# Scheduler thresholds as a string of settings along the run, in a planned attention and MLP kernel

## The chip, the cores and the metric

The kernel runs on one core of one Trainium2 chip. The metric is the device time of one execution in microseconds (us). Three runs of the kernel before gave 1594.99, 1595.41 and 1596.77 us; the median, 1595.41, is the time before.

The engines are named as in the profile: PE is TensorE (matrix products; PEld is its loading of weights), ACT is ScalarE, DVE is VectorE, POOL is GpSimd and SP is SyncE, which issues the DMAs.

## What is computed

The reference, cut to what matters. The sequence has 2048 tokens of 512 values, and there are 32 heads of 16 values.

```python
def _A_ref(x, wqkv, wo):
    H = 32; Dh = D // H
    qkv = (x @ wqkv).reshape(B, S, 3, H, Dh).transpose(2, 0, 3, 1, 4)
    q, k, v = qkv[0], qkv[1], qkv[2]
    p = _softmax(jnp.einsum("bhqd,bhkd->bhqk", q, k) * Dh ** -0.5)
    o = jnp.einsum("bhqk,bhkd->bhqd", p, v)
    return o.transpose(0, 2, 1, 3).reshape(B, S, D) @ wo

def _B_ref(x, w1, b1, w2, b2):               # w1: 512 x 1376, w2: 1376 x 512
    h = _gelu(jnp.einsum("bsd,df->bsf", _layernorm(x), w1) + b1)
    return jnp.einsum("bsf,fd->bsd", h, w2) + b2

x = x + _A_ref(_layernorm(x), wqkv, wo)
x = x + _B_ref(_layernorm(x), w1, b1, w2, b2)
x = x + _A_ref(_layernorm(x), wqkv, wo)
x = x + _B_ref(_layernorm(x), w1, b1, w2, b2)
```

Each attention needs an exponential of 32 x 2048 x 2048 scores. In tiles of 128 keys by 512 queries of one head that is 16 x 4 x 32 = 2048 tiles, and 4096 for both.

## The kernel before

**A planner writes the program.** The Python code doesn't list the instructions of each engine in order. It runs a list scheduler, `Sched`, over a model of the chip: every operation has a duration, and every engine a time at which it is free (`P.free`). Jobs are generators that yield tasks with a priority (a lower number goes first). `Sched.run` picks, over and over, the task that can start first (`best`, L389), and appends its instructions to the engine's stream. The streams are then emitted with the semaphore waits that the dependences need. So the order on each engine is fixed when the program is built, and the thresholds at L477 to L509 are arguments of that planning: they are read by the planner and are not on the chip. A change of one threshold at one point can change the order of all that follows.

**Segments and tiles.** The attention is cut into segments (`build_segments`): one block of queries for one group of four heads. A segment has its score tiles, and the tiles of the key blocks in `DK` (3, 6, 9, 12 and 15) are kept in a list of their own, `todod`, because they may go to DVE. These are 5 of 16 key blocks, 1280 of the 4096 tiles.

**Two ways to an exponential.** ACT takes groups of tiles. `flow_scores` (L1319) forms them by turns with three tiles (PSUM banks 0 to 2) and two tiles (banks 3 and 4); before the run is `wide`, in the first part, both have two. PE writes the scores of a group (L1401), ACT reads all banks of it in one instruction (L1386) and writes bf16 probabilities into one of nine sets of `PT` (five with three tiles, four with two). The counter `gi` numbers the groups. DVE takes a tile alone: an addition of a constant to the score, rounded to a 16-bit integer, gives the bits of an approximate exponential (`d_load`, L1478). Two such tiles share one buffer `dp`, and three more additions (`job_d`, L1509) make copies shifted by quarter powers of two. All four copies are multiplied with V scaled to match (`vs`), which averages the error out. A tile on ACT thus needs one product with V, and a tile on DVE four.

**Which tile goes to DVE** is decided by `take_d` (L1411). It needs DVE not too far behind, room in `dp`, a free PSUM bank (bank 5, `DLANE`, or bank 7, `MISCB`), and a tile in `todod` whose operands are there. It is asked in three places: by `flow_scores` beside each group, by `d_solo` after each DVE instruction that is planned (L1458, when the DVE work at hand is at most `D_IDLE`), and when PE has a gap. Tiles of `todod` that nobody has taken when a segment's other tiles are done go to ACT.

**Products with V** are batched by `try_pv` (L1526). It considers probabilities that are ready within `PV_NEAR`, takes one or two from each of the four heads, and gives the batch a value: the number taken over 4 (r + 0.5), with r the depth, at most 2. If the value is below `PV_LEAST` it holds the batch back, until PE has been drained for `PV_IDLE` (0.5 us), a set of `PT` is lacking (`starved`), or the segment's last tiles are due.

**Scores go first on PE.** When a score task is expected soon, `scores_due` (L417) gives a due time, and `best` passes over any other PE task that would drain more than `HOLD_LATE` after it.

**Linear layers** (QKV L927, output projection L1658, the MLP L1713 and L1756) run beside the attention, at their own priorities, in pieces of two matmuls; products with V have priority 1.0 and scores 0.0. They share PSUM bank 7.

When all is planned, `refill` (L1202) goes through the plan once more and puts matmuls with a tile of zeros (`zw`, L1307, L1309, L1311) into PE's gaps.

Of the kernel before, what the change touches and what calls it, by code (L numbers as in the profile page):

```python
# [38 lines left out]
DK = (3, 6, 9, 12, 15)  # L39
# [239 lines left out]
class Sched:  # L279
# [137 lines left out]
    def scores_due(self, f, lim):  # L417

        first = None
        for t in self.pend["pe"]:  # L420
            if t.prio == 0.0:
                r = self.task_ready(t)
                if r > lim and (first is None or r < first):
                    first = r
        if first is None or first - f > HOLD_REACH:
            return None
        act = self.P.free["act"] + sum(max(0.02, o[4] - OVERLAP["act"]) for t in self.pend["act"] for o in t.ops)
        return max(first, act - HOLD_LEAD) + HOLD_LATE

    def drained(self, task, t):  # L430

# [45 lines left out]
AHEAD = 0.3  # L477
HOLD_REACH = 1.0
HOLD_LEAD = 0.45
HOLD_LATE = 0.4  # L480
FILL_GAP = 0.2
FILL_LEAST = 96
FILL_MOST = 448
# [6 lines left out]
GELU_FROM = 0.3  # L490
GELU_TO = 0.5
DLANE = 5
D_IDLE = 1.2
D_NEAR = 0.5
D_PRIO = 0.5
DBATCH = 2
# [5 lines left out]
MISCB = 7  # L502
DTAIL = 8
DURGE = 8
PV_NEAR = 0.7
PV_DEEP = 2
PV_COST = 0.5
PV_LEAST = 0.75
PV_IDLE = 0.5  # L509


class Builder:
# [380 lines left out]
    def job_qkv_tile(self, L, tt, slot, i, left, prio, what):  # L893
        S_ = self.S_
# [8 lines left out]
        xnT, RXT = self.xnT[:, xs, :, :], ("xnT", xs)  # L903
# [20 lines left out]

        def mm(which, b):
            for c0 in (0, 2):
                yield Task("pe", prio, [I(lambda e, c=c: e.matmul(self.ps[:, b, :], lhsT=xnT[:, c, :], rhs=self.wqkv[:, c, which * 512:which * 512 + 512], start=(c == 0), stop=(c == 3)),  # L927
                                          [("wqkv", which), RXT], [("ps", b)], 0.216, [("ps", b)]) for c in (c0, c0 + 1)])
        yield ("ready", "pe", [RXT])
        if "k" in what:  # L930
# [388 lines left out]
    def flow_scores(self):  # L1319
# [4 lines left out]
        self.batch = None  # L1324
        self.ptuse = {}
        self.lane_busy = False
        self.dload = 0
        for b in range(4):
            S_.retire("mb", b, ("ret", b))
        last = {}  # L1330
        while True:
            self.advance()
            if self.cur == len(self.segs):
                break
# [35 lines left out]
            while self.wide and len(grp) + len(dts) < 4:  # L1370
                d = self.take_d([s_["tiles"][j][1] for s_, j in grp] + [s_["tiles"][j][1] for s_, j, b, bt, w in dts])
                if d is None:
                    break
                dts.append(d)
            ops = []
            for (sg, j), b in zip(grp, banks):
                ops.append(self.score(sg, j, b))
# [30 lines left out]
        while self.cur < len(self.segs) and not self.left(self.segs[self.cur]):  # L1408
            self.cur += 1

    def take_d(self, hps):  # L1411

        S_, P = self.S_, self.P
        self.advance()
        if self.cur == len(self.segs) or self.dload > 1 or P.free["dve"] - S_.now > 1.3 or sum(o[4] for t in S_.pend["dve"] for o in t.ops) > DBACK:
            return None
        if self.batch is None and (not S_.pools["dp"].free or S_.pools["dp"].waiters or self.flying >= DFLY):
            return None
        mb = S_.pools["mb"]
        soon = lambda b: P.ready("pe", (), [("ps", b)]) <= max(S_.now, P.free["pe"]) + 0.1  # L1420
        if not self.lane_busy and ("ret", DLANE) in S_.done and soon(DLANE):
            b = DLANE
        elif MISCB in mb.free and not mb.waiters and soon(MISCB):
            b = MISCB
        else:
            return None
        sg = self.segs[self.cur]
        if self.left(sg) < DTAIL:
            if self.cur + 1 == len(self.segs):
                return None  # L1430
            sg = self.segs[self.cur + 1]
            if sg["nt"] - self.left(sg) >= (DAHEAD if ("retq", 5) in S_.done else DAHEAD // 2):
                return None
        if not sg["todod"]:
            return None
        j = next((j for j in sg["todod"] if sg["tiles"][j][1] not in hps), sg["todod"][0])
        kbs = sg["tiles"][j][0]
        if not all(k in self.S_.done for k in [("qt", sg["i"])] + self.kv_keys(sg, kbs) + [("vs", sg["i"], kb) for kb in kbs]):
            return None
        if b == DLANE:  # L1440
            self.lane_busy = True
        else:
            mb.free.remove(b)
        self.dload += 1
        sg["todod"].remove(j)
        sg["n"] += len(SHIFT) - 1
        bt = self.batch
        if bt is None:
            bt = self.batch = {"unit": S_.pools["dp"].free.pop(0), "tiles": [], "loaded": 0, "closed": False}
            self.ptuse[("dp", bt["unit"])] = 1  # L1450
            self.flying += 1
        w = len(bt["tiles"])
        bt["tiles"].append((sg, j))
        if w + 1 == DBATCH:
            self.batch = None
        return (sg, j, b, bt, w)

    def d_solo(self):  # L1458

        S_ = self.S_  # L1460
        if not self.wide or self.P.free["dve"] - S_.now + sum(o[4] for t in S_.pend["dve"] if S_.task_ready(t) <= S_.now + D_NEAR for o in t.ops) > D_IDLE:
            return
        d = self.take_d([])
        if d is not None:
# [61 lines left out]
    def try_pv(self):  # L1526
        S_ = self.S_
        while True:
# [2 lines left out]
            sg = self.segs[self.acc_seg]  # L1531
            if self.pv_out >= (1 if self.pv_first else 2) or not sg["rdy"]:
                return
            near = [it for it in sg["rdy"] if self.P.last_writer[it[2]].t1 <= S_.now + PV_NEAR]
            if len(near) < len(sg["rdy"]):
                S_.seq += 1
                heapq.heappush(S_.timers, (min(self.P.last_writer[it[2]].t1 for it in sg["rdy"] if it not in near) - PV_NEAR + 0.01, S_.seq, self.try_pv))
            if not near:
                return
            by = defaultdict(list)  # L1540
# [124 lines left out]
    def job_post(self, L, qc):  # L1665
# [43 lines left out]
    def mm_w1(self, L, qc, fc, b, pr, W, off=0):  # L1709
        M = 128 if fc < self.NFC - 1 else self.FLAST  # L1710
        yield ("keys", [("w1", L, qc, fc)])
        for c0 in (0, 2):
            yield Task("pe", pr, [I(lambda e, c=c: e.matmul(self.ps[0:M, b, off:off + W], lhsT=self.w1(fc, c), rhs=self.yT[:, c, 0:W], start=(c == 0), stop=(c == 3)),  # L1713
                                    [("wf", fc)] + [("yT", i) for i in range(W // 128)], [("ps", b)], 0.216 * W / 512, [("ps", b)]) for c in (c0, c0 + 1)])

    def gt(self, fc, i, W):
# [4 lines left out]
    def job_ffn(self, L, qc):  # L1721
# [30 lines left out]
        for i, tt in enumerate(tiles):  # L1752
            yield ("ready", "pe", GR + [r for fc in range(NFC) for r in self.w2res(L, fc)])
            b = yield ("get", "mb")
            for f0 in range(0, NFC, 2):
                yield Task("pe", pr, [I(lambda e, fc=fc, i=i, b=b: e.matmul(self.ps[:, b, :], lhsT=self.gt(fc, i, W), rhs=self.w2(L, fc), start=(fc == 0), stop=(fc == nf)),  # L1756
                                        GR + self.w2res(L, fc), [("ps", b)], 0.216, [("ps", b)]) for fc in range(f0, min(f0 + 2, NFC))])
            S_.submit(Task("dve", pr - 0.7, [I(lambda e, tt=tt, b=b: e.tensor_tensor(out=self.xres[:, tt, :], in0=self.ps[:, b, :], in1=self.xres[:, tt, :], op=ALU.add), [("ps", b), ("x", tt)], [("x", tt)], 0.68)]),
                      cb=lambda b=b, tt=tt: self.x_done(L, tt, b, pr))
# [179 lines left out]
```

## Time and profile before

| | |
|---|---|
| median of three runs | 1595.41 us |
| the profiled execution's own time | 1595.76 us |
| its span, first to last instruction | 1594.1 us |
| PE busy, with the zero matmuls | 1538.6 us (97%) |
| ACT busy | 1528.0 us (96%) |
| DVE busy | 1450.3 us (91%) |
| POOL busy | 333.9 us (21%) |
| exponential groups on ACT | 1274, first at 24.8 us, last at 1571.3 us |
| tiles on DVE | 944, first at 90.3 us, last at 1558.8 us |

A row for a group of instructions has the line, the engine and the operation, then what it writes and reads with the shapes, the count, the busy time in us, the mean duration of one in ns, and last the idle time of the engine just before these instructions with what ended it. A row of waits has the engine and line that waited, the one waited for, and the time in total, how often, and the longest. A row of the timeline begins with the start and the busy time of a run of equal instructions; in brackets is the idle time before it.

### The profile page before, as it was taken

To read this page: it belongs to the slowest core of one execution; us is meant where nothing else is said; L and a number is where in the kernel's file an instruction comes from. 1 tells how busy PE (TensorE), PEld (TensorE's weight loads), DVE (VectorE), ACT (ScalarE), POOL (GpSimd) and SP (SyncE) were. 2 spreads that over 40 slices of the span, in tenths; PEclk is the share of its full clock that TensorE was granted. 3 is DMA by queue.
4 is the path that set the end of the run, shared out by engine and by line. 5 is a ranking of instruction groups with operands and counts; after the bars stand their busy time and mean duration, and the time that the engine had idled before them with its cause. 6 is when DMAs were issued, how large, how long until landed. Compare 5 with 4: busy or idle time off the path is not lost.

```text
span 1594.1 us, 39159 instructions
## 1 busy us (share of the span) xinstructions
PE 1538.6 (97%) x16364; PEld 479.4 (30%) x16497; DVE 1450.3 (91%) x3202; ACT 1528.0 (96%) x1357; POOL 333.9 (21%) x574
## 2 busy tenths in 40 slices
PE   9999999999999999999999999999999999999998
PEld 3222222222222222222222223222222222344444
DVE  7689999989999899989999898999899989999793
ACT  6999999999999999989999998999999999999996
POOL 5585312001220012103212217310001000020010
PEclk9999999999999999999999999999999999999999
DMA  6662012112321223223722233211101100221100
GB/s 172 116 142 87 29 31 40 48 41 59 81 48 50 44 53 78 57 53 86 139 44 62 53 68 78 61 25 21 34 14 38 28 19 22 40 48 30 41 25 21
DMA packets 212465, 88.80 MB, mean 56 GB/s; under 512 B 183835, under 2 KB 206656, under 8 KB 212288
## 3 DMA queue, kind: packets, MB, share of 16 engines
q1 hardware_dynamic: 212288, 86.29, 24.0%
q8 instruction: 129, 2.11, 0.6%
q14 instruction: 48, 0.39, 0.1%
HBM read 34.65 MB, written 19.48 MB: 34 GB/s over the span
## 4 chain that ended last, share of the span: by engine, by line
PE 51%; DVE 28%; ACT 17%; issue 2%; POOL 0%; DMA 0%; POOLq 0%; DVEq 0%
PE ps L1401 18%; ACT PT L1386 15%; PE ps L1579 15%; DVE dp L1478 12%; DVE dp L1509 9%; PE ps L1713 4%; PE ps L1756 4%; PE ps L927 3%; PE ps L1307 3%; ACT h L1748 1%; PE ps L1311 1%; PE ps L1658 1%; DVE accT L1609 1%; DVE st L850 1%; DVE n L992 1%
## 5 line engine op out<-in xcount | busy, mean ns | idle before, releaser
L1386 ACT ACTIVATE PT<-ps 128x1536 bf16<-128x1536 f32 (+1 forms) x1274 | 1449.7, 1259 | 38.8 <-PE ps L1401 32.2
L1401 PE MATMUL ps<-QT,KT 32*128 32x512 bf16 (+1 forms) x4608 | 672.3, 358 | 16.8 <-DVE dp L1478 5.5
L1478 DVE TENSOR_SCALAR dp<-ps 128x512 uint16<-128x512 f32 x944 | 632.6, 681 | 61.2 <-PE ps L1401 58.2
L1509 DVE TENSOR_SCALAR dp<-dp 128x1024 uint16<-128x1024 uint16 (+1 forms) x1434 | 557.4, 430 | 7.9 <-PE ps L1579 3.2
L1579 PE MATMUL ps<-PT,V 128*17 128x512 bf16 (+1 forms) x3544 | 467.1, 358 | 0.0
L1579 PE MATMUL ps<-dp,vs 128*17 128x512 bf16 (+1 forms) x3192 | 444.4, 357 | 0.5 <-DVE dp L1509 0.2
L1401 PEld LDWEIGHTS ps<-QT,KT 32*128 32x128 bf16 x4608 | 172.2, 91 | 546.4 <-ACT PT L1386 237.3
L1144 POOL TENSOR_SCALAR QT<-qraw,scl,qbias 128x512 bf16<-128x512 bf16 (+1 forms) x84 | 72.2, 860 | 790.0 <-PE ps L1401 784.8
L1579 PE MATMUL ps<-dp,V 128*17 128x512 bf16 (+1 forms) x1064 | 215.3, 357 | 1.3 <-DVE accT L1609 1.0
L1309 PE MATMUL ps<-zw 32*128 32x444 bf16 (+5 forms) x702 | 193.5, 323 | 0.0
L1579 PEld LDWEIGHTS ps<-dp,vs 128*17 128x17 bf16 x3192 | 111.0, 88 | 130.3 <-issue 106.8
L1579 PEld LDWEIGHTS ps<-PT,V 128*17 128x17 bf16 x3544 | 113.2, 88 | 102.5 <-issue 89.6
L1311 PE MATMUL ps<-zw 128*32 128x448 bf16 (+22 forms) x1477 | 136.5, 323 | 0.4 <-DVE dp L1478 0.2
L1307 PE MATMUL ps<-zw 128*128 128x448 bf16 (+17 forms) x481 | 114.1, 333 | 4.0 <-DVE ps L727 1.7
L1713 PE MATMUL ps<-yT,wf 128*128 128x512 bf16 (+3 forms) x353 | 92.9, 356 | 8.6 <-issue 4.4
L927 PE MATMUL ps<-wqkv,xnT 128*128 128x512 bf16 x299 | 85.8, 382 | 7.6 <-issue 3.5
L1609 DVE STREAM_TRANSPOSE accT<-ps 128x512 f32<-128x512 f32 (+1 forms) x88 | 57.9, 658 | 10.8 <-PE ps L1579 9.9
L1737 DVE TENSOR_SCALAR h<-ps,b1c 128x512 bf16<-128x512 f32 (+2 forms) x88 | 62.3, 708 | 5.0 <-PE ps L1713 4.7
L1579 PEld LDWEIGHTS ps<-dp,V 128*17 128x17 bf16 x1064 | 53.1, 88 | 45.2 <-issue 27.3
L1169 POOL TENSOR_SCALAR vs<-V 128x340 bf16<-128x340 bf16 (+2 forms) x72 | 60.5, 842 | 26.3 <-PE ps L1579 21.2
L1307 PEld LDWEIGHTS ps<-zw 128*128 128x128 bf16 x481 | 37.4, 98 | 74.2 <-issue 46.4
L1311 PEld LDWEIGHTS ps<-zw 128*32 128x32 bf16 x1477 | 49.1, 95 | 22.1 <-DVE dp L1478 4.1
(179 smaller groups left out, 892.2 us busy)
## 6 DMA issues: line engine op xcount, KB each, us to landing
vs<-vs_scr SPq DMA_DIRECT2D x56, 255.0 KB, 2.8
wf<-in_B_w_dram SPq DMA_DIRECT2D x90, 128.0 KB, 2.6
q_scr<-qk SPq DMA_DIRECT2D x22, 256.0 KB, 2.1
k_scr<-qk SPq DMA_DIRECT2D x12, 256.0 KB, 2.0
out_dram<-xres SPq DMA_DIRECT2D x16, 128.0 KB, 1.7
vs_scr<-vs SPq DMA_DIRECT2D x8, 255.0 KB, 2.9
xres<-in_A_x_dram SPq DMA_DIRECT2D x7, 256.0 KB, 3.3
v_scr<-vst SPq DMA_DIRECT2D x12, 136.0 KB, 1.7
```

The costliest lines, as they stand in the source:

```text
L927: yield Task("pe", prio, [I(lambda e, c=c: e.matmul(self.ps[:, b, :], lhsT=xnT[:, c, :], rhs=self.wqkv[:, c, which * 512:which * 512 + 512 ...
L1144: yield Task(eng, 0.4, [I(lambda e: e.tensor_scalar(out=self.QT[:, q, 0:W], in0=src, scalar1=self.scl[:, k, hg:hg + 1], scalar2=self.qbias ...
L1307: fn = lambda e: e.matmul(self.ps[:, b, 0:w], lhsT=self.zw[:, 0:128], rhs=self.zw[:, 0:w], start=st, stop=st, skip_group_check=True)
L1309: fn = lambda e: e.matmul(self.ps[:, b, 0:w], lhsT=self.zw[32 * p:32 * p + 32, 0:128], rhs=self.zw[32 * p:32 * p + 32, 0:w], start=st, sto ...
L1311: fn = lambda e: e.matmul(self.ps[32 * p:32 * p + 32, b, 0:w], lhsT=self.zw[:, 0:32], rhs=self.zw[:, 0:w], start=st, stop=st, skip_group_c ...
L1386: S_.submit(Task("act", 1e-5 * gi, [I(lambda e, pt=pt, n=n, b0=b0: e.activation(out=self.PT[:, pt:pt + n, :], in_=self.ps[:, b0:b0 + n, :] ...
L1401: return [I(lambda e, kb=kb, i=i: e.matmul(self.ps[:, b, i * W:(i + 1) * W], lhsT=self.KT[32 * hp:32 * hp + 32, hg, kb * 128:(kb + 1) * 12 ...
L1478: self.S_.submit(Task("dve", 0.0, [I(lambda e: e.tensor_scalar(out=self.dp[:, u, w * 512:(w + 1) * 512], in0=self.ps[:, b, :], scalar1=BIT ...
L1509: yield Task("dve", pr, [I(lambda e, k=k, v=v: e.tensor_scalar(out=self.dp[:, v, 0:N], in0=self.dp[:, u, 0:N], scalar1=float(SHIFT[k]), sc ...
L1579: ops.append((nth[j, sh] + 0.1 * i, I(lambda e, hp=hp, v=v, ap=ap[:, i * W:(i + 1) * W], first=first and i == 0, W=W: e.matmul(self.ps[32 ...
L1609: yield Task("dve", 0.3, [I(lambda e: e.transpose(self.accT[:, a, 0:W], self.ps[:, ACCB, 0:W]), [("ps", ACCB)], [RA], 0.17 + 0.535 * W / 5 ...
L1713: yield Task("pe", pr, [I(lambda e, c=c: e.matmul(self.ps[0:M, b, off:off + W], lhsT=self.w1(fc, c), rhs=self.yT[:, c, 0:W], start=(c == 0 ...
```

## The change

Four thresholds, `HOLD_LATE`, `D_IDLE`, `PV_NEAR` and `PV_LEAST`, become attributes of an object `HINT`. `flow_scores` sets them anew at every eighth group from a string with one digit for each eight groups. The digit 0 stands for the values before; each of the nine others changes one value.

| digit | value | its steps |
|---|---|---|
| 1 | `D_IDLE` 0.8 (was 1.2) | 128 |
| 2 | `D_IDLE` 1.7 | 9, 141 |
| 3 | `PV_LEAST` 0.6 (was 0.75) | 88, 100 |
| 4 | `PV_LEAST` 0.9 | 43, 65, 96, 125, 143, 153, 159 |
| 5 | `HOLD_LATE` 0.2 (was 0.4) | 1, 2, 32, 74, 104, 149 |
| 6 | `HOLD_LATE` 0.6 | none |
| 7 | `PV_NEAR` 0.4 (was 0.7) | 10, 17, 80, 122, 138 |
| 8 | `LIN2` 0.9 (base 9) | 151, 155 |
| 9 | `D_STEAL` 1.0 (base 0) | 25, 110 |

The string has 160 digits, 27 of which are not 0. Two of the values are new:

- `LIN2`: the pieces of a linear layer's tile after the first get the lower of their priority and `LIN2`. With 9 that is the priority they had.
- `D_STEAL`: a group of three for which `take_d` gave no tile, while the DVE work at hand (`dve_work`) is below `D_STEAL`, gives its third bank to a DVE tile. The group's third tile goes back to the front of its list, and ACT's instruction has two tiles. The bank comes free when DVE has loaded the tile. `dve_work` is DVE's free time minus now plus the pending work that is ready within 0.5 us; the base value is 0.

```diff
-        return max(first, act - HOLD_LEAD) + HOLD_LATE
+        return max(first, act - HOLD_LEAD) + HINT.HOLD_LATE
...
+class Hint:
+    BASE = dict(D_IDLE=1.2, PV_LEAST=0.75, HOLD_LATE=0.4, PV_NEAR=0.7, LIN2=9, D_STEAL=0)
+    MODES = ({}, dict(D_IDLE=0.8), dict(D_IDLE=1.7), dict(PV_LEAST=0.6), dict(PV_LEAST=0.9), dict(HOLD_LATE=0.2), dict(HOLD_LATE=0.6), dict(PV_NEAR=0.4), dict(LIN2=0.9), dict(D_STEAL=1.0))
+    STEP = 8
+    ORDER = '0550000002700000070000000900000050000000000400000000000000000000040000000050000070000000300000004000300050000090000000000070040010000000007002040000050804080004'
...
+    def at(self, step):
+        self.mode(int(self.ORDER[step]) if step < len(self.ORDER) else 0)
...
+            if gi % Hint.STEP == 0:
+                HINT.at(gi // Hint.STEP)
...
+            if self.wide and not dts and len(grp) in (3,) and self.dve_work() < HINT.D_STEAL:
+                d = self.take_d([s_["tiles"][j][1] for s_, j in grp[:-1]], banks[-1])
+                if d is not None:
+                    sg, j = grp.pop()
+                    (sg["todod"] if set(sg["tiles"][j][0]) <= set(DK) else sg["todo"]).insert(0, j)
+                    last[banks.pop()] = ("lane", gi)
+                    self.lanes[d[2]] = ("lane", gi)
+                    self.cur = min(self.cur, sg["i"])
+                    self.nsteal += 1
+                    dts.append(d)
...
+    def dve_work(self):
+        S_ = self.S_
+        return self.P.free["dve"] - S_.now + sum(o[4] for t in S_.pend["dve"] if S_.task_ready(t) <= S_.now + D_NEAR for o in t.ops)
...
-    def take_d(self, hps):
+    def take_d(self, hps, lane=None):
...
-        if not self.lane_busy and ("ret", DLANE) in S_.done and soon(DLANE):
+        if lane is not None:
+            b = lane
+        elif not self.lane_busy and ("ret", DLANE) in S_.done and soon(DLANE):
             b = DLANE
...
-        if not self.wide or self.P.free["dve"] - S_.now + sum(o[4] for t in S_.pend["dve"] if S_.task_ready(t) <= S_.now + D_NEAR for o in t.ops) > D_IDLE:
+        if not self.wide or self.dve_work() > HINT.D_IDLE:
...
+        elif b in self.lanes:
+            self.S_.mark(("free", self.lanes.pop(b)))
...
-            near = [it for it in sg["rdy"] if self.P.last_writer[it[2]].t1 <= S_.now + PV_NEAR]
+            near = [it for it in sg["rdy"] if self.P.last_writer[it[2]].t1 <= S_.now + HINT.PV_NEAR]
...
-            if value(r) < PV_LEAST and not self.starved and len(near) < sg["n"] - sg["sub"]:
+            if value(r) < HINT.PV_LEAST and not self.starved and len(near) < sg["n"] - sg["sub"]:
...
-                yield self.oproj_mm(b, i, (h0, h0 + 1), 128, pr)
+                yield self.oproj_mm(b, i, (h0, h0 + 1), 128, pr if h0 == 0 else min(pr, HINT.LIN2))
```

The priority of the later pieces is changed in the same way in the QKV product and in both products of the MLP.

More of the change, by code (lines that the diff above doesn't have):

```diff
@@ L479 @@
 HOLD_LEAD = 0.45
-HOLD_LATE = 0.4
 FILL_GAP = 0.2
@@ L492 @@
 DLANE = 5
-D_IDLE = 1.2
 D_NEAR = 0.5
@@ L504, with mode @@
 DURGE = 8
-PV_NEAR = 0.7
 PV_DEEP = 2
 PV_COST = 0.5
-PV_LEAST = 0.75
 PV_IDLE = 0.5
+class Hint:
[3 more added lines that the diff above has]
+    ORDER = '0550000002700000070000000900000050000000000400000000000000000000040000000050000070000000300000004000300050000090000000000070040010000000007002040000050804080004'
+    def mode(self, k):
+        self.__dict__.update(self.BASE)
+        self.__dict__.update(self.MODES[k])
+    def at(self, step):
+        self.mode(int(self.ORDER[step]) if step < len(self.ORDER) else 0)
+HINT = Hint()
+HINT.mode(0)
 class Builder:
@@ L926, in mm @@
             for c0 in (0, 2):
-                yield Task("pe", prio, [I(lambda e, c=c: e.matmul(self.ps[:, b, :], lhsT=xnT[:, c, :], rhs=self.wqkv[:, c, which * 512:which * 512 + 512], start=(c == 0), stop=(c == 3)),
+                yield Task("pe", prio if c0 == 0 else min(prio, HINT.LIN2), [I(lambda e, c=c: e.matmul(self.ps[:, b, :], lhsT=xnT[:, c, :], rhs=self.wqkv[:, c, which * 512:which * 512 + 512], start=(c == 0), stop=(c == 3)),
                                           [("wqkv", which), RXT], [("ps", b)], 0.216, [("ps", b)]) for c in (c0, c0 + 1)])
@@ L1326, in flow_scores @@
         self.lane_busy = False
+        self.lanes = {}
+        self.nsteal = 0
         self.dload = 0
@@ L1441, in take_d @@
             self.lane_busy = True
-        else:
+        elif lane is None:
             mb.free.remove(b)
@@ L1533, in try_pv @@
                 return
-            near = [it for it in sg["rdy"] if self.P.last_writer[it[2]].t1 <= S_.now + PV_NEAR]
+            near = [it for it in sg["rdy"] if self.P.last_writer[it[2]].t1 <= S_.now + HINT.PV_NEAR]
             if len(near) < len(sg["rdy"]):
                 S_.seq += 1
-                heapq.heappush(S_.timers, (min(self.P.last_writer[it[2]].t1 for it in sg["rdy"] if it not in near) - PV_NEAR + 0.01, S_.seq, self.try_pv))
+                heapq.heappush(S_.timers, (min(self.P.last_writer[it[2]].t1 for it in sg["rdy"] if it not in near) - HINT.PV_NEAR + 0.01, S_.seq, self.try_pv))
             if not near:
@@ L1712, in mm_w1 @@
         for c0 in (0, 2):
-            yield Task("pe", pr, [I(lambda e, c=c: e.matmul(self.ps[0:M, b, off:off + W], lhsT=self.w1(fc, c), rhs=self.yT[:, c, 0:W], start=(c == 0), stop=(c == 3)),
+            yield Task("pe", pr if c0 == 0 else min(pr, HINT.LIN2), [I(lambda e, c=c: e.matmul(self.ps[0:M, b, off:off + W], lhsT=self.w1(fc, c), rhs=self.yT[:, c, 0:W], start=(c == 0), stop=(c == 3)),
                                     [("wf", fc)] + [("yT", i) for i in range(W // 128)], [("ps", b)], 0.216 * W / 512, [("ps", b)]) for c in (c0, c0 + 1)])
@@ L1755, in job_ffn @@
             for f0 in range(0, NFC, 2):
-                yield Task("pe", pr, [I(lambda e, fc=fc, i=i, b=b: e.matmul(self.ps[:, b, :], lhsT=self.gt(fc, i, W), rhs=self.w2(L, fc), start=(fc == 0), stop=(fc == nf)),
+                yield Task("pe", pr if f0 == 0 else min(pr, HINT.LIN2), [I(lambda e, fc=fc, i=i, b=b: e.matmul(self.ps[:, b, :], lhsT=self.gt(fc, i, W), rhs=self.w2(L, fc), start=(fc == 0), stop=(fc == nf)),
                                         GR + self.w2res(L, fc), [("ps", b)], 0.216, [("ps", b)]) for fc in range(f0, min(f0 + 2, NFC))])
```

## The prediction

> **What bounds the kernel now.** I read the engine totals first, then the groups by shape, the waits, and the timeline of ACT and DVE.
>
> ```profile
> PE 1538.6 (97%) x16364; PEld 479.4 (30%) x16497; DVE 1450.3 (91%) x3202; ACT 1528.0 (96%) x1357; POOL 333.9 (21%) x574
> L1309 PE MATMUL ps<-zw 32*128 32x444 bf16 (+5 forms) x702 | 193.5, 323 | 0.0
> L1311 PE MATMUL ps<-zw 128*32 128x448 bf16 (+22 forms) x1477 | 136.5, 323 | 0.4 <-DVE dp L1478 0.2
> L1307 PE MATMUL ps<-zw 128*128 128x448 bf16 (+17 forms) x481 | 114.1, 333 | 4.0 <-DVE ps L727 1.7
> ```
>
> PE's 97% is not a limit: three groups multiply by the zero tile `zw`, filler that the planner puts into gaps. The limit is ACT at 96%, with DVE second. ACT's busy time, by shape, is nearly all exponentials:
>
> ```profile
> L1386 ACT ACTIVATE PT<-ps 128x1536 bf16<-128x1536 f32 x605 | 897.1, 1483 | 21.0 <-PE ps L1401 14.9
> L1386 ACT ACTIVATE PT<-ps 128x1024 bf16<-128x1024 f32 x668 | 700.8, 1057 | 17.8 <-PE ps L1401 17.4
> L1478 DVE TENSOR_SCALAR dp<-ps 128x512 uint16<-128x512 f32 x944 | 632.6, 681 | 61.2 <-PE ps L1401 58.2
> L1509 DVE TENSOR_SCALAR dp<-dp 128x1024 uint16<-128x1024 uint16 x1398 | 548.9, 433 | 7.6 <-PE ps L1579 2.9
> ```
>
> 605 groups of three tiles, 668 of two and one single make 3152 tiles on ACT; 944 go to DVE; 4096 in all. The durations overlap, so the price of a tile comes from runs of the timeline:
>
> ```profile
> 24.77 15.91 ACT L1386 ACTIVATE PT<-ps 128x1024 bf16<-128x1024 f32 x17 [2.69 <-PE ps L1401]
> 462.31 38.07 ACT L1386 ACTIVATE PT<-ps 128x1536 bf16<-128x1536 f32 x33 [0.41 <-PE ps L1401]
> 961.75 11.43 ACT L1386 ACTIVATE PT<-ps 128x1024 bf16<-128x1024 f32 x10 [4.36 <-PE ps L1401]
> 1557.46 1.23 DVE L1478 TENSOR_SCALAR dp<-ps 128x512 uint16<-128x512 f32 x2
> 1559.41 3.09 DVE L1509 TENSOR_SCALAR dp<-dp 128x1024 uint16<-128x1024 uint16 x9
> ```
>
> A group of two costs 15.91/17 = 0.936 us. 33 alternating groups take 38.07, so a group of three costs about (38.07 - 16.5 x 0.936)/16.5 = 1.371. One tile more or less on ACT is therefore 0.435 us, and a group itself about 0.936 - 2 x 0.435 = 0.066.
>
> What ACT does not use is 66 us of 1594.1. Busy time by stretches says where:
>
> ```profile
> 0.00:30.00 30.00, 27.52 (x158) 12.08 (x163) 23.02 (x70) 16.96 (x27) 18.77 (x55) 1.00 0.63 176
> 100.00:1560.00 1460.00, 1415.24 (x15479) 434.47 (x15599) 1366.43 (x3011) 1426.78 (x1239) 269.42 (x451) 1.00 0.22 50
> 1560.00:1594.00 34.00, 27.89 (x251) 13.71 (x252) 9.61 (x23) 18.76 (x26) 1.48 (x4) 0.98 0.10 24
> ```
>
> (The stretch and its length, then PE, weight loads, DVE, ACT, POOL, the granted clock, the DMA share and GB/s.) Of ACT's idle time 30 - 16.96 = 13.0 us lie ahead of the exponentials and 34 - 18.76 = 15.2 in the tail, where the settings have no exponential groups left to order; 1460 - 1426.78 = 33.2 lie between 100 and 1560, and DVE has 1460 - 1366.43 = 93.6 there. The waits name the cause:
>
> ```profile
> ACT PT L1386 <- PE ps L1401: 32.2, 80, 4.4
> DVE dp L1478 <- PE ps L1401: 58.2, 81, 3.0
> ```
>
> ACT waits 32.2 us for scores, 80 times, 0.40 us on average. DVE waits almost twice that, also for scores: 0.72 us each time. So two stocks can be drawn on: ACT's stalls, one for one, and DVE's idle time, through tiles that move from ACT to DVE.
>
> **The change part by part.** No setting puts an instruction on the chip; all of it reorders the plan, and moves tiles between ACT and DVE.
>
> (1) *The steal.* It stands in every group, not in two windows only. The base has `D_STEAL=0`, and the test is `dve_work() < 0`; that sum is negative when DVE has already run dry (its free time lies before now) and nothing is about to be ready. So a three-tile group that got no DVE tile gives up its last one when DVE idles: that is the situation of the 81 waits. Roughly half of the groups are wide, so I count 40 steals. Each takes the group from 1.371 to 0.936, but the returned tile is done later by ACT unless the DVE tile is a net addition. Net additions follow from DVE time. A stolen tile's score goes out ahead of the group (priority -0.5), so I let it save half the wait: 40 x 0.72 / 2 = 14.4 us of DVE. The price of a tile there: a load of 1.23/2 = 0.615 plus three shifts, each shared by two tiles, 3 x (3.09/9)/2 = 0.515, together 1.13. That is 12.7 tiles, say 12: ACT -12 x 0.435 = -5.2. The other 28 steals only split groups: 28/2.5 = 11 more groups x 0.066 = +0.7. Sum -4.5. PE pays three more V products per net tile, 3 x 0.21/4 = 0.16 us (0.21 is the spacing of L1579's waves in the timeline, at 954.53, 954.75 and 954.96, four products side by side), 2 us in all, taken from filler. The steal adds one wait: the next wide group gets its third bank only when DVE has loaded the tile, 0.681 after its score, where it used to wait for a group of 1.371; with DVE idle that is earlier, so nothing; if DVE is late, the scores stand behind it on PE, and ACT behind them. Bounds: no net tile, 40/2.5 x 0.066 = +1.1; every wait filled, 58.2/1.13 = 51 tiles = -22.
>
> [...] The rows above have two loads in 1.23 and nine shifts in 3.09, less than the durations added up, so I take 1.13.
>
> The two windows with `D_STEAL=1.0` allow 4 wide groups each, at most 8 tiles or -3.5; the DVE rows there show 0.9 us idle in the first and nothing in the second, so DVE only takes them earlier: -0.5.
>
> (2) *The settings.* 27 of 160 steps are not base. Counting L1386's groups per 10 us places each: step 1 at 32 us, step 96 at 954 to 967, step 155 near 1530. They cover 255 us. The ACT idle rows inside them add up to 7.9 us, 4.36 of it the stall at 961.75, ahead of the second attention's first scores. Directly they can win 7.9; what they cost, at one mean wait of 0.40 for each of 27, is +10.8. Since a list planner's later order shifts after every nudge, the other stalls also move (670 to 750 us holds 0.68, 1.26, 1.74, 1.40 and 1.18), up or down. I take half the direct stock, -4.0, nearest to the row of 4.36: this is the judgement in the sum. By kind: `HOLD_LATE` 0.2 holds PE work back from a due score (for ACT, against DVE's evictions); `PV_NEAR` 0.4 and `PV_LEAST` 0.6 change batch sizes; `D_IDLE` moves solo loads by 0.4 to 0.5 us; `LIN2` lets the rest of a linear pass V products at two places near the end. Each alone is worth between -0.4 and +0.4.
>
> `PV_LEAST` 0.9, at seven steps, is another matter: the value of a batch is at best 8/(4 x 2.5) = 0.8, so under it V products go only when PE has idled 0.5 us, a PT set runs out, or the segment ends. [...] This trace grants 1.00 up to 1560 us and 0.98 in the tail, and the 0.5 us limit with the filler keeps gaps short; I take nothing.
>
> (3) Code loading, DMAs, queues: nothing added. SP's loads move only with the order; the ones that ACT could wait for do not appear among its waits, so nothing.
>
> **Sum**: -4.5 - 0.5 - 4.0 = -9.0 on the profiled span of 1594.1. Around it lie 1595.76 - 1594.1 = 1.7, and that execution is 0.35 above the median; so 1595.41 - 9.0 = 1586.4, 0.56% faster.
>
> **Rivals.**
> *DVE's wait is filled* (0.13): 80% of the 58.2 us at 1.13 is 41 tiles, -18, and -4 from stalls: 1573.5. For it: 336 (1280 - 944) tiles of the DVE blocks are still done by ACT, so there is supply. Against: DVE is 91% busy, and its batches and two spare banks limit it.
> *One half only* (0.15): steals or settings give nothing on the chip: about 1591.
> *No change* (0.10): DVE tiles come earlier but not more of them, and the stalls reappear elsewhere: 1595. For it: the settings' 255 us hold only 7.9 us of ACT idle time, so there is little where they act. Against: the steal acts in every group.
> *Slower, V products held too long* (0.10): place, the seven `PV_LEAST` 0.9 windows of some 9.5 us. ACT writes into nine PT sets, about nine groups x 1.154 = 10.4 us, so the sets run out at a window's end; then a score waits for a batch of V products. If each window costs 9.0/7 = 1.3 us of ACT the gain is gone, from 1.7 us on it is measurably slower; at 2 us, 1600.
>
> **How the numbers follow.** What a measurement here can tell is about 0.2%, 3.2 us. The likeliest case has 0.52, with a range of its own of 1581 to 1591. Faster: 0.52 + 0.13 + 0.15 = 0.80; same 0.10; slower 0.10. The range takes in half of the filled-DVE case and the no-change case with the foot of the slower one: 1574 to 1597.
>
> **What would show it.** Right: L1478's count rises from 944 by 8 to 20, ACT's exponentials fall by as many tiles (fewer of 1536, more of 1024), DVE's wait for L1401 falls from 58 to about 45, ACT's busy time by 4 to 5 and its wait by about 4. Wrong: the L1478 count unchanged (no net steals); L1386's wait above 32 with PE's L1579 as what runs before it (V products held); clock below 1.00 between 100 and 1560; a stall at the second attention's start longer than 4.4.

## The result and the profile after

The changed kernel takes 1584.08 us (median of four runs, 1583.48 to 1584.76), against 1595.97 us for the kernel before in the same comparison. The ratio is 0.9926, with a 95% interval of 0.9909 to 0.9943: 0.74% faster. The prediction said 1586.4.

The engine totals of the changed kernel, its exponentials and DVE tiles by shape (as before: count, busy us and mean ns, idle time ahead), and the two waits that the prediction named. Lines have moved: L1414 is the exponential, L1429 the scores, L1512 and L1545 the two DVE steps, L1615 the products with V.

```profile
PE 1549.1 (98%) x16223; PEld 471.7 (30%) x16223; DVE 1450.7 (92%) x3210; ACT 1524.5 (96%) x1362; POOL 332.3 (21%) x574
```

```profile
L1414 ACT ACTIVATE PT<-ps 128x1536 bf16<-128x1536 f32 x593 | 882.1, 1487 | 14.9 <-PE ps L1429 9.6
L1414 ACT ACTIVATE PT<-ps 128x1024 bf16<-128x1024 f32 x685 | 718.0, 1063 | 15.3 <-PE ps L1429 14.6
L1512 DVE TENSOR_SCALAR dp<-ps 128x512 uint16<-128x512 f32 x946 | 631.8, 679 | 60.4 <-PE ps L1429 57.9
```

```profile
DVE dp L1512 <- PE ps L1429: 57.9, 80, 4.3
ACT PT L1414 <- PE ps L1429: 24.2, 62, 2.7
```

The span fell from 1594.1 to 1581.7, by 12.4 us. ACT accounts for it in two terms. Its idle time went from 1594.1 - 1528.0 = 66.1 to 1581.7 - 1524.5 = 57.2 (-8.9), its busy time fell by 3.5. DVE's tiles went from 944 to 946 only, and DVE's wait for scores stayed at 58 us: the second stock of the prediction was not touched.

ACT by four stretches, the kernel before and then the changed one (stretch, its length, ACT busy, the clock, DMA):

```profile
0.00:100.00 100.00, 82.50 (x94) 1.00 0.67 145
100.00:550.00 450.00, 443.54 (x390) 1.00 0.21 52
550.00:980.00 430.00, 409.47 (x351) 1.00 0.33 73
980.00:1550.00 570.00, 563.86 (x493) 1.00 0.15 32
```

```profile
0.00:100.00 100.00, 82.79 (x94) 1.00 0.60 136
100.00:550.00 450.00, 442.89 (x391) 1.00 0.23 54
550.00:980.00 430.00, 414.91 (x360) 1.00 0.35 74
980.00:1550.00 570.00, 566.32 (x497) 1.00 0.14 32
```

Between 550 and 980 us, where the linear layers of one block lead over to the second attention, ACT's idle time fell from 20.5 to 15.1 (-5.4), behind it from 6.1 to 3.7 (-2.5), and after 1550 us from 15.4 to 14.1 (-1.4). Before 550 nothing was won (24.0 us before, 24.3 after). The longest stalls of this stretch show the same in the changed kernel's timeline: the 4.36 us ahead of the second attention's scores has become 1.73.

```profile
720.55 16.15 ACT L1414 ACTIVATE PT<-ps 128x1024 bf16<-128x1024 f32 x14 [1.55 <-PE ps L1429]
899.01 4.73 ACT L1414 ACTIVATE PT<-ps 128x1024 bf16<-128x1024 f32 x4 [1.44 <-PE ps L1429]
955.32 5.54 ACT L1414 ACTIVATE PT<-ps 128x1024 bf16<-128x1024 f32 x5 [1.73 <-PE ps L1429]
```

### The profile page after: what moved, and what is told of

The parts are those of the page before. It is cut to its first block, busy times and chain, and to the rows that moved or that the text cites. A ratio compares the mean times of both kernels' runs of the same rounds, so it can differ in the third digit from the quotient of the medians.

```text
span 1581.7 us, 38782 instructions
## 1 busy us (share of the span) xinstructions
PE 1549.1 (98%) x16223; PEld 471.7 (30%) x16223; DVE 1450.7 (92%) x3210; ACT 1524.5 (96%) x1362; POOL 332.3 (21%) x574
## 4 chain that ended last, share of the span: by engine, by line
PE 54%; DVE 23%; ACT 20%; issue 2%; POOL 0%; SPq 0%; DMA 0%; POOLq 0%; DVEq 0%
ACT PT L1414 19%; PE ps L1429 19%; PE ps L1615 16%; DVE dp L1512 10%; DVE dp L1545 7%; PE ps L1749 5%; PE ps L1792 4%; PE ps L941 4%; PE ps L1321 3%; PE ps L1694 1%; DVE accT L1645 1%; PE ps L1325 1%; PE ps L1323 1%; ACT h L1784 1%; DVE n L1006 1%
## 5 line engine op out<-in xcount | busy, mean ns | idle before, releaser
L1414 ACT ACTIVATE PT<-ps 128x1536 bf16<-128x1536 f32 (+1 forms) x1279 | 1445.8, 1259 | 30.2 <-PE ps L1429 24.2
L1512 DVE TENSOR_SCALAR dp<-ps 128x512 uint16<-128x512 f32 x946 | 631.8, 679 | 60.4 <-PE ps L1429 57.9
L1429 PE MATMUL ps<-QT,KT 32*128 32x512 bf16 (+1 forms) x4608 | 672.3, 358 | 13.9 <-DVE dp L1512 5.2
L1545 DVE TENSOR_SCALAR dp<-dp 128x1024 uint16<-128x1024 uint16 x1440 | 558.2, 427 | 6.1 <-PE ps L1615 1.7
L1615 PE MATMUL ps<-PT,V 128*17 128x512 bf16 (+1 forms) x3540 | 468.9, 358 | 0.1
L1615 PE MATMUL ps<-dp,vs 128*17 128x512 bf16 (+1 forms) x3204 | 438.5, 357 | 0.9 <-DVE dp L1545 0.9
L1429 PEld LDWEIGHTS ps<-QT,KT 32*128 32x128 bf16 x4608 | 172.1, 91 | 546.6 <-ACT PT L1414 258.5
L1615 PE MATMUL ps<-dp,V 128*17 128x512 bf16 (+1 forms) x1068 | 212.5, 357 | 2.7 <-DVE accT L1645 2.1
L1323 PE MATMUL ps<-zw 32*128 32x444 bf16 (+4 forms) x697 | 189.2, 322 | 0.0
L1615 PEld LDWEIGHTS ps<-dp,vs 128*17 128x17 bf16 x3204 | 111.4, 88 | 118.8 <-issue 97.0
L1615 PEld LDWEIGHTS ps<-PT,V 128*17 128x17 bf16 x3540 | 112.9, 88 | 112.6 <-issue 99.4
L1321 PE MATMUL ps<-zw 128*128 128x448 bf16 (+13 forms) x475 | 113.7, 335 | 2.9 <-DVE ps L741 1.7
L1325 PE MATMUL ps<-zw 128*32 128x448 bf16 (+24 forms) x1202 | 111.7, 320 | 0.3 <-DVE dp L1512 0.2
L1749 PE MATMUL ps<-yT,wf 128*128 128x512 bf16 (+3 forms) x396 | 101.7, 360 | 1.6 <-DVE accT L1645 0.8
L941 PE MATMUL ps<-wqkv,xnT 128*128 128x512 bf16 x336 | 95.3, 383 | 1.6 <-DVE qy L1013 0.4
L1615 PEld LDWEIGHTS ps<-dp,V 128*17 128x17 bf16 x1068 | 52.4, 88 | 43.9 <-issue 23.1
L882 POOL TENSOR_SCALAR xn<-xres,rs,nmr 128x512 bf16<-128x512 bf16 x54 | 53.4, 996 | 10.6 <-DMA xnT<-xn 5.1
```

What stands on the lines that cost most here:

```text
L941: yield Task("pe", prio if c0 == 0 else min(prio, HINT.LIN2), [I(lambda e, c=c: e.matmul(self.ps[:, b, :], lhsT=xnT[:, c, :], rhs=self.wqk ...
L1321: fn = lambda e: e.matmul(self.ps[:, b, 0:w], lhsT=self.zw[:, 0:128], rhs=self.zw[:, 0:w], start=st, stop=st, skip_group_check=True)
L1323: fn = lambda e: e.matmul(self.ps[:, b, 0:w], lhsT=self.zw[32 * p:32 * p + 32, 0:128], rhs=self.zw[32 * p:32 * p + 32, 0:w], start=st, sto ...
L1325: fn = lambda e: e.matmul(self.ps[32 * p:32 * p + 32, b, 0:w], lhsT=self.zw[:, 0:32], rhs=self.zw[:, 0:w], start=st, stop=st, skip_group_c ...
L1414: S_.submit(Task("act", 1e-5 * gi, [I(lambda e, pt=pt, n=n, b0=b0: e.activation(out=self.PT[:, pt:pt + n, :], in_=self.ps[:, b0:b0 + n, :] ...
L1429: return [I(lambda e, kb=kb, i=i: e.matmul(self.ps[:, b, i * W:(i + 1) * W], lhsT=self.KT[32 * hp:32 * hp + 32, hg, kb * 128:(kb + 1) * 12 ...
```

## The experiments

Two theories stood against each other. **M**, the prediction's: each part has a worth of its own (the steal brings tiles to DVE, each setting helps the groups it stands at). **P**: the parts have hardly any worth; each nudge throws the list planner onto another complete plan, and the string is one path picked among many.

For P there is a number that can be had before a run: the planner's own end, the time at which the last operation ends in the model that orders the work. It is 1590.5 for the kernel before and 1577.9 for the changed one. It is no measurement, and the runs show how far it carries. Other counts that are said below to be of the plan are taken in the same way, while the program is built.

**The steal alone.**

```diff
-    ORDER = '0550000002700000070000000900000050000000000400000000000000000000040000000050000070000000300000004000300050000090000000000070040010000000007002040000050804080004'
+    ORDER = '0' * 160
```

> All 160 digits are 0: the thresholds stay at the base, and only the steal with its base threshold acts. Theory M (each part of the change has a worth of its own, as the prediction summed it): the steal is worth 4.5 us, so about 1591, with 8 to 20 more tiles on DVE. Theory P (the settings have no worth of their own; they nudge the planner onto another complete plan, and the string is one picked path): the steal alone is just another nudge. The planner's own end of its plan, which for the two known kernels lay 5.4 and 6.2 us under the measured time, moves by only +0.4 us against before and has 3 more DVE tiles, so 1596, no change.

Measured: 1599.37 us, ratio 1.0022 (1.0015 to 1.0030), slower than before. DVE loads 947 tiles, three more than before, and its wait is still 57.8 us. ACT's idle time is 70.7, 4.6 more than before. So the steal, taken alone, gains nothing, and M's 1591 fell. P's "no change" was nearer, but it isn't the measured time either.

**The string without the steal.**

```diff
-    BASE = dict(D_IDLE=1.2, PV_LEAST=0.75, HOLD_LATE=0.4, PV_NEAR=0.7, LIN2=9, D_STEAL=0)
+    BASE = dict(D_IDLE=1.2, PV_LEAST=0.75, HOLD_LATE=0.4, PV_NEAR=0.7, LIN2=9, D_STEAL=-1e9)
...
-    ORDER = '0550000002700000070000000900000050000000000400000000000000000000040000000050000070000000300000004000300050000090000000000070040010000000007002040000050804080004'
+    ORDER = '0550000002700000070000000000000050000000000400000000000000000000040000000050000070000000300000004000300050000000000000000070040010000000007002040000050804080004'
```

> The string with its two digits 9 set to 0, and a threshold that never steals: the settings alone. Theory M: the settings keep their worth, 4 to 8 us, so 1588 to 1592. Theory P: without the steals the same settings meet other plans, and almost nothing is left; the planner's own end moves by -0.9 us against before, so about 1595.

Measured: 1595.76 us, ratio 0.9998 (0.9988 to 1.0008): no change. Neither half alone gives any of the 11.9 us. Only the plan that both make together has them.

**One digit fewer.**

```diff
-    ORDER = '0550000002700000070000000900000050000000000400000000000000000000040000000050000070000000300000004000300050000090000000000070040010000000007002040000050804080004'
+    ORDER = '0500000002700000070000000900000050000000000400000000000000000000040000000050000070000000300000004000300050000090000000000070040010000000007002040000050804080004'
```

> The changed kernel with one of its 27 digits set back to 0: step 2, HOLD_LATE 0.2 for eight groups near 40 to 47 us, in a stretch where ACT has 0.4 us of idle time. Theory M: one setting of 27 is worth 0.4 us, so 1584 to 1585, still faster than before. Theory P: all that follows is planned anew by settings that were picked for another plan, and the whole gain goes: the planner's own end is 19.1 us above the changed kernel's, 6.4 above before, so about 1602, slower than before.

Measured: 1606.65 us, ratio 1.0063 (1.0040 to 1.0086). One setting for eight groups near 40 us, taken away, costs some 22 us (10.4 above before, where the changed kernel is 11.9 below); eight groups that last some 8 us in all cannot hold an effect of that size. This is the run that decides between M and P. Waits of that kernel:

```profile
DVE dp L1512 <- PE ps L1429: 58.7, 96, 2.5
ACT PT L1414 <- PE ps L1429: 38.4, 89, 3.5
```

ACT waits 38.4 us for scores, 14 more than in the changed kernel, in 89 places instead of 62; between 550 and 980 us its idle time is 21.8. DVE's wait is as before.

**The same digits at other places**, twice.

```diff
+    ORDER = '0500004000000000803400900000000002000900000000050500000000400000050400000000000004000000040005100700070000000000700000003000000000070000000004075002000000000080'
```

> The same 27 digits and the steal, in a random order over the 160 steps. Theory M: the same settings as often as before save about as much, 1584 to 1590. Theory P: a random path, which can come out on either side; the planner's own end is 11.1 us above before, so about 1607.

Measured: 1611.00 us in two runs, ratio 1.0092 (1.0063 to 1.0122).

```diff
+    ORDER = '0000000700000000000000000000000000000000040004009070700005000050000500070240000094000000000700000304001000000005000803040000002000000500000008000000000000005400'
```

> The same 27 digits in a second random order, one of those whose plan ends early. Theory M: 1584 to 1590, as for the first random order. Theory P: the planner's own end is 1.8 us under before, so 1594 to 1598; together with the first random order it shows how far apart two strings with the same settings lie.

Measured: 1597.31 us, ratio 1.0010 (1.0000 to 1.0020). The same 27 settings and the same steal give 1584, 1597 and 1611 us. What they are doesn't determine the time; where they stand does. ACT waits 41.9 and 39.5 us for scores in these two.

**The steal wherever it can be had.** It was the prediction's largest single term, so its stock deserved a direct test.

```diff
+    ORDER = '9' * 160
```

> All 160 digits are 9 (D_STEAL 1.0): the steal as often as it can be had, 98 times in the plan instead of 14, with 975 tiles on DVE instead of 944. Theory M (the prediction's first term): 31 net tiles at 0.435 us less on ACT are 13.5 us, less 67/2.5 x 0.066 = 1.8 for more groups, so about 1584. Theory P: the tiles move, but what ACT saves on them it waits for elsewhere; the planner's own end is 1.0 us above before, so 1597 to 1600, with ACT's exponentials some 11 us shorter and its idle time as much longer.

Measured: 1595.92 us, ratio 1.0001 (0.9991 to 1.0011). Its DVE tiles, and its waits:

```profile
L1512 DVE TENSOR_SCALAR dp<-ps 128x512 uint16<-128x512 f32 x975 | 647.7, 679 | 42.7 <-PE ps L1429 39.8
```

```profile
ACT PT L1414 <- PE ps L1429: 40.5, 97, 5.8
DVE dp L1512 <- PE ps L1429: 39.8, 51, 3.3
```

Here the stock was drawn on: 31 more tiles, and DVE's wait fell from 58 to 40. ACT's busy time fell by 8.0 (1528.0 to 1520.0). But its wait for scores rose by 8.3 (32.2 to 40.5), and its idle time from 66.1 to 73.0. Between 550 and 980 us it is 24.6 instead of 20.5. The tiles moved as planned and the time stayed the same. That ACT's saved work turned into waiting for scores is what these numbers suggest. They don't show it: this is one plan, and plans with equal digits differ by up to 27 us. The plan with the steal alone is 3 us slower than this one, with 28 tiles fewer on DVE.

**Products with V held back in the whole run**, the prediction's slower rival.

```diff
+    ORDER = '4' * 160
```

> All 160 digits are 4: PV_LEAST 0.9, which no batch of V products can reach, so they go out only when PE has been idle, a PT set is lacking or the segment ends. The prediction's slower rival gives this a price of some 2 us for eight groups once the PT sets run out, which over the run would be far above 100 us; if it costs nothing the time stays near 1596. Theory P has the planner's own end 12.5 us above before: 1606 to 1612, with ACT's wait for scores well above 32 us.

Measured: 1613.03 us in two runs, ratio 1.0103 (1.0083 to 1.0123). The kernel is 16.1 us slower, with ACT's wait for scores at 48.0. For eight groups that is 16.1/160 = 0.1 us, a twentieth of the price that the rival was given. It is not that PT sets run out more rarely: in the plan a set is lacking at 159 of 1278 groups, about once in eight groups as the rival had it (49 of 1279 in the changed kernel). So each time costs far less. How much of the 16.1 us is due to holding back stays open, since a mere reordering of the 27 digits cost 14.8.

**A tight due time in the whole run.**

```diff
+    ORDER = '5' * 160
```

> All 160 digits are 5: HOLD_LATE is 0.2 in the whole run. Theory M: a tighter due time is good for the scores, and it is six of the settings; everywhere it saves at least what it does there, so 1588 or less, with ACT's wait for scores clearly under 32 us. Theory P: one more path; the planner's own end is 4.6 us under before, but plans that were not picked on the chip came out 3 to 4 us worse than their plan, so 1592 to 1596.

Measured: 1599.99 us, ratio 1.0025 (1.0018 to 1.0033). ACT waits 40.5 us for scores, in 45 places. The longest wait is a fifth of that, and stands where the groups of three begin:

```profile
92.97 9.29 ACT L1414 ACTIVATE PT<-ps 128x1536 bf16<-128x1536 f32 x8 [8.59 <-PE ps L1429]
```

So M's 1588 fell. It isn't shown that the setting harms the scores: in the profiled execution, the fastest of 18, ACT is idle for 32.6 us between 100 and 1550 us, where the kernel before has 33.1, and this version also has the steal, which alone took 1599.37 us. P's number missed too: an end 4.6 us earlier was planned, 4.1 later was measured.

**The first 40 digits.**

```diff
-    ORDER = '0550000002700000070000000900000050000000000400000000000000000000040000000050000070000000300000004000300050000090000000000070040010000000007002040000050804080004'
+    ORDER = '0550000002700000070000000900000050000000000000000000000000000000000000000000000000000000000000000000000000000000000000000000000000000000000000000000000000000000'
```

> The string's first 40 digits (7 settings, up to 330 us), then zeros. Theory M: 7 of 27 settings give a quarter of the settings' share, and the steal its 4.5, so about 1590. Theory P: the choice of the first path decides, since the later plan follows from it; the planner's own end is 8.4 us under before, so 1588 to 1592, and the time is not won in the first 330 us, but behind them, where no threshold differs from the base.

Measured: 1594.10 us (1591.32 to 1597.29 in 18 runs), ratio 0.9991 (0.9983 to 0.9998). Most of the planned 8.4 us did not arrive; in the profiled execution (span 1590.5) ACT's idle time between 550 and 980 us is 14.9, as low as in the changed kernel, and 9.1 instead of 3.7 behind it. So a good middle can follow from early digits alone, and a poor end after it takes much of it back.

**Without the five settings of the middle.** Do settings work where they stand?

```diff
-    ORDER = '0550000002700000070000000900000050000000000400000000000000000000040000000050000070000000300000004000300050000090000000000070040010000000007002040000050804080004'
+    ORDER = '0550000002700000070000000900000050000000000400000000000000000000000000000000000000000000000000000000300050000090000000000070040010000000007002040000050804080004'
```

> The changed kernel with the digits of steps 65, 74, 80, 88 and 96 set to 0: all five settings between 550 and 980 us, the stretch in which ACT's idle time fell most, from 20.5 to 15.1 us. If settings work where they stand, these 5.4 us go back: about 1589.5. If the gain there is inherited from the plan that the first settings left behind (theory P), nothing changes: the planner's own end is 0.2 us later, so 1583.5 to 1585, and the idle time between 550 and 980 us stays near 15.

Measured: 1586.54 us (1583.36 to 1588.42), ratio 0.9935 (0.9916 to 0.9953). The idle time between 550 and 980 us is 430 - 414.23 = 15.8, not 20.5. So 4.7 of the 5.4 us won there do not come from the five settings that stand there. The stall ahead of the second attention's scores, 4.36 us in the kernel before, is short here too, though the setting of step 96, which stood at it, is gone:

```profile
958.19 11.40 ACT L1414 ACTIVATE PT<-ps 128x1024 bf16<-128x1024 f32 x10 [1.81 <-PE ps L1429]
```

This run shows something else. Up to step 65 the program is the changed kernel's: the two plans are equal on every engine up to 635 us. Yet ACT is idle for 9.2 us between 100 and 550 us where the changed kernel has 7.1. The difference arises near 275 us; two stretches of each, the changed kernel first (PE, weight loads, DVE, ACT, POOL, clock, DMA share and GB/s):

```profile
270.00:275.00 5.00, 4.91 (x59) 1.29 (x59) 5.00 (x13) 5.00 (x6) 2.08 (x2) 1.00 0.52 106
275.00:280.00 5.00, 4.22 (x42) 1.36 (x41) 4.28 (x12) 4.65 (x5) 0.00 (x0) 1.00 0.30 81
```

```profile
270.00:275.00 5.00, 4.91 (x59) 1.32 (x59) 5.00 (x13) 5.00 (x6) 2.85 (x4) 1.00 0.56 107
275.00:280.00 5.00, 3.12 (x20) 0.76 (x18) 2.62 (x7) 2.88 (x3) 0.00 (x0) 0.66 0.38 104
```

And the matmul at which it begins, in each, from the timeline of PE:

```profile
275.78 0.59 PE L1749 MATMUL ps<-yT,wf 128*128 128x512 bf16 x2 [0.78 <-DVE accT L1645]
```

```profile
276.92 0.63 PE L1749 MATMUL ps<-yT,wf 128*128 128x512 bf16 x1 [1.88 <-DMA yT<-xn]
```

The MLP's first product waits for the transposing DMA of `yT`. In the second execution the matmul began 1.14 us later, behind the DMA, and the scores that are planned after it on PE came later too. Within this gap of 1.88 us the granted clock fell: by the microsecond it is 0.73, 0.50, 0.50 and 0.57 from 276 to 280 us, then 1.00 again. The three L1749 matmuls there took 631 ns each, where those of the changed kernel took 379 in the median. ACT then waited 2.12 us for scores.

What made the DMA late stands in POOL's timeline, the changed kernel first:

```profile
263.85 0.28 POOL L872 TENSOR_SCALAR rs<-mv 128x4 f32<-128x4 f32 x1 [13.54 <-DVE mv L865]
```

```profile
263.90 2.62 POOL L872 TENSOR_SCALAR rs<-mv 128x4 f32<-128x4 f32 x1 [13.54 <-DVE mv L865]
```

The same small instruction of the layer norm began at the same time and took 2.62 us instead of 0.28. POOL's later steps, which make `xn`, moved with it, and SP issued the first transpose of `yT` at 269.19 us instead of 267.68. Why the instruction took so long is not shown.

**A string searched further.** With single to fourfold random changes of the digits, kept when the planner's own end came earlier:

```diff
+    ORDER = '0550120202701007090589886986000650072046070495570611672700507000850817865755888005767004077760807805356551979690000060588776245510002002087042142502150849193714'
```

> A string searched further from the change's own, by random changes of one to four digits that were kept when the planner's own end came earlier; 112 of its 160 digits are not 0. Its plan ends 1.4 us earlier than the changed kernel's. If the plan were a true measure of the chip, 1582.7. The runs so far lie 4.4 to 14 us behind their plans, and the changed kernel with 6.2 is among the nearest; a plan picked by its own end alone should fall back towards the middle of these, 8 us, so 1584 to 1587, not better than the changed kernel.

Measured: 1587.14 us, ratio 0.9946 (0.9928 to 0.9964), no better than the changed kernel. Its four runs have mean granted clocks of 0.998, 0.998, 0.997 and 0.993, and took 1585.83, 1586.63, 1587.64 and 1591.66 us: the lower the clock, the longer. The profiled one is the last; in it the clock breaks down three times (means over 5 us of 0.75 from 180 us, 0.81 from 275 and 0.50 from 475), most near 480 us:

```profile
470.00:475.00 5.00, 3.53 (x25) 0.69 (x26) 3.07 (x10) 3.41 (x4) 0.00 (x0) 0.77 0.51 82
475.00:480.00 5.00, 5.00 (x26) 0.88 (x29) 2.78 (x6) 2.62 (x3) 0.00 (x0) 0.50 0.09 26
480.00:485.00 5.00, 4.67 (x28) 0.75 (x22) 2.71 (x5) 3.53 (x4) 0.00 (x0) 0.50 0.08 26
485.00:490.00 5.00, 5.00 (x40) 1.11 (x39) 3.87 (x9) 3.91 (x4) 0.00 (x0) 0.87 0.08 26
```

ACT is idle for 20 - 13.47 = 6.5 us of these 20. Here the clock of 0.50 lasts nearly 14 us, an estimate from the four means: if it is either 1.00 or 0.50, it is at 0.50 for (0.23 + 0.50 + 0.50 + 0.13) x 5/0.50 = 13.6 us. Again a wait of L1749 for `yT` stands at the beginning, 1.37 us, and again a long L872 ahead of it:

```profile
458.96 2.29 POOL L872 TENSOR_SCALAR rs<-mv 128x4 f32<-128x4 f32 x1 [14.67 <-DVE mv L865]
```

The same instruction took 2.63 us at 264.21, ahead of the second breakdown, at 278 us, where PE is idle for 2.04 us between 275 and 280. The first, near 182 us, stands behind five microseconds in which PE was busy for 4.89.

**The same plan with more filler.**

```diff
-FILL_U = 0.55
+FILL_U = 0.75
```

> The plan of the further-searched string, with the filler's target FILL_U raised from 0.55 to 0.75: 686 more matmuls by the zero tile in PE's gaps (16742 PE instructions instead of 16056), the same order of all other work and the same planned end. If that plan lost its 1.4 us to the PE clock (granted 0.993 to 0.998 in its four runs, with half clock for some 10 us near 480 us), the clock now stays at 1.00 and the time is 1582 to 1584. If the waits for late DMAs cost it, and the clock only shows them, the time stays at 1586 to 1588; if the filler gets in the way of scores, it is longer.

Measured: 1585.04 us in five runs (1583.51 to 1585.86), ratio 0.9929 (0.9915 to 0.9942). The clocks are now 0.998 to 1.000 and the breakdown near 480 us is not there; 1.7 us came back (9.8 below before, then 11.5). The intervals of the two runs overlap, and it isn't shown that the filler is what held the clock. In the profiled execution L872 took 0.28 us at 264 and again at 457, PE waited for no DMA of `yT` at either place, and it has no gap at 470 us (busy 5.00 of 5.00 up to 475): what stood ahead of the breakdown was itself missing. The time lies between the two that were expected, 1582 to 1584 if the clock took all that was missing, and 1586 to 1588 if the late DMAs did. The plan has 546 zero matmuls more (16742 weight loads against 16196), not 686; the 16056 of the expectation are the PE records of the earlier trace, some of which are missing. This version doesn't beat the changed kernel (0.9926); none of the versions did.

How the planned end stands to the chip, over all runs (changes against the kernel before, us; measured as the difference of the medians in one comparison):

| kernel | planned | measured |
|---|---|---|
| the change | -12.6 | -11.9 |
| steal alone | +0.4 | +3.1 |
| string without the steal | -0.9 | -0.5 |
| without step 2 | +6.4 | +10.4 |
| other places, first | +11.1 | +14.8 |
| other places, second | -1.8 | +1.4 |
| steal everywhere | +1.0 | 0.0 |
| first 40 digits | -8.4 | -1.8 |
| due time 0.2 everywhere | -4.6 | +4.1 |
| V products held everywhere | +12.5 | +16.1 |
| without the middle five | -12.4 | -10.4 |
| searched further | -14.0 | -9.8 |
| the same, more filler | -14.0 | -11.5 |

The planner puts the kernels roughly in order, within -1 to +9 us. Differences of 1 or 2 us in the plan, which is what a further search finds, are below that.

## Why the prediction was right, and where not

The sum was right (1586.4 against 1584.08; -9.0 predicted, -11.9 measured) and its terms were not, so the hit was luck. The prediction's own signs say the same. DVE's tiles rose by 2 and not by 8 to 20, and its wait stayed at 58 us where 45 was expected. ACT's wait fell by 8.0, twice what was expected.

**What bounds the kernel**: right. All of the gain in the span is ACT's, 8.9 us of idle time and 3.5 of busy time.

**(1) The steal, -5.0**: wrong. The step that failed is the net addition of 12 tiles from 40 steals. The plan has 14 steals, the trace two more tiles (-0.9 us by the price of a tile, +0.3 for five more groups), and taken alone the part is slower. The count of 40 took DVE's waits on the chip for idle time that the planner sees. In the plan 423 of 607 groups of three get no DVE tile at first, but `dve_work` is below its threshold at only 23 of them, and `take_d` then gives a tile at 14. The assumption under the term, that a tile less on ACT is time won one for one, found no support either: the run with 31 more tiles on DVE took as long as the kernel before. The price per tile, 1.13 us by the timeline's rows, therefore decided nothing.

**(2) The settings, -4.0**: right in sign, too small, and not for the reason given. I counted the idle time inside the settings' own windows and took half of it. But of the 5.4 us of idle time that ACT lost between 550 and 980 us, 4.7 stay lost when the five settings there are taken out, with them most of the fall of the stall of 4.36; and one setting at 40 us, removed, costs some 22. The prediction said in a clause that the later order shifts after every nudge; that clause was the main effect, and the windows were the wrong stock. The stock was ACT's whole wait for scores, and no run gives a way to work out the draw from it by a setting.

**The busy time, -3.5**: near the 4 to 5 that were foreseen, but not by the tiles that were to give it. Tiles and groups give -0.5. A stall also costs the overlap of the next exponential with the one before it: counted group by group in the two traces, one that starts behind a gap adds about 0.11 us more to ACT's busy time than one in a run (1.02 against 0.92 for two tiles, 1.44 against 1.33 for three), and 23 fewer start behind a gap (165 instead of 188). That is 2.5 us. It is argued from these counts, not tested, and 0.5 us are left over.

**The clock**: I took nothing for it, and in the changed kernel that was right (1.00 between 100 and 1550 us). Products with V held back were no danger to it either: with `PV_LEAST` 0.9 in the whole run it is at 1.00 as well. For the neighbours nothing was too little. Without the middle five a clock of 0.50 came with a gap of 1.88 us that a late DMA had made, and in the string searched further it came behind one of 1.37 us. But in these runs the length of a gap alone doesn't decide it. With the tight due time in the whole run L1749 waited 1.53 us for the same kind of DMA, and the clock stayed at 1.00; with the second random order it fell where PE had been busy almost throughout:

```profile
492.35 0.38 PE L1749 MATMUL ps<-yT,wf 128*128 128x512 bf16 x1 [1.53 <-DMA yT<-xn]
490.00:495.00 5.00, 3.47 (x31) 0.80 (x30) 2.73 (x6) 4.00 (x4) 1.03 (x1) 1.00 0.22 47
```

```profile
1410.00:1415.00 5.00, 4.97 (x78) 2.58 (x78) 4.09 (x9) 4.42 (x5) 0.56 (x1) 0.68 0.07 16
```

What does decide it stays open.

**The rivals**: the filled wait of DVE was realised in part, by the steal everywhere, and that plan won nothing; V products held back cost about a twentieth of the price given, as far as one plan shows it. "One half only" fell as well, since either half alone is nothing or worse.

What stays open: why this plan has fewer late scores than its neighbours. That it has is measured; no single wait or setting was found that makes it so.

## What to carry to other kernels

In this list planner a threshold was a way of choosing another plan more than a change with an effect of its own, so its forecast is a spread. Here the same 27 settings in three orders gave 1584, 1597 and 1611 us. Estimate the spread from the time that the bounding engine waits (ACT's 24 to 48 us over all versions here), not from the place where the threshold acts, and choose among plans by measuring, since the model's last 1 to 2 us do not carry over. Don't count work taken off the bounding engine as won before it is measured: here 8 us less of it came with 7 us more of waiting. And when one program takes different times, follow a late DMA back to the engine that fed it: here it was one small instruction on an engine that is 21% busy.

## What the runs showed of the hardware

- One POOL instruction of 128x4 values took 0.28 us in one execution and 2.62 us in another with the same order of work up to there; in the further-searched version it took 2.63 and 2.29 us at two places, and 0.28 at both with more filler. Behind the one of 2.62 us the first transpose was issued 1.51 us later, and PE waited 1.88 us for the DMA (0.78 us, for DVE, in the changed kernel); behind the one of 2.29 us PE waited 1.37 us.
- A wait of 1.88 us on PE for a late DMA came with a granted clock of 0.66 over five microseconds and matmuls of 631 ns instead of 379; one of 1.37 us was followed by ten microseconds at a mean of 0.50 (nearly 14 us by the estimate above); beside one of 1.53 us the clock stayed at 1.00.
- Plans differ in how steady they are. 51 executions of the kernel before, in one comparison, lie within 1594.87 to 1597.09, all at a mean clock of 1.00; 18 of the plan with a tight due time lie between 1596.74 (clock 1.000) and 1607.33 (0.993), and 18 with the first 40 digits between 1591.32 (1.000) and 1597.29 (0.996). The lost clock goes with the longer time.
